# Decode attention with a gated feed-forward part: the heads' turning one wo block sooner, and the last wo row as two column halves

## The chip, the cores and the metric

The kernel runs on one core of a Trainium2 chip. The metric is the device time of one execution in microseconds (us); a lower time is better. Faster or slower needs 2%, which is 27 us here.

Two clocks occur below. The time of a run is 1.8 to 2.1 us longer than the span of its profile, which goes from the first to the last instruction. Moments in the text are microseconds from the span's start.

## The reference, cut to what matters

```python
q = (x @ wq).reshape(B, Sq, H, Dh).transpose(0, 2, 1, 3)      # B=4, Sq=1, D=1024, H=32, Dh=128
scores = jnp.einsum("bhqd,bhkd->bhqk", q, k_cache) * (Dh ** -0.5)   # k_cache: 4 x 32 x 8192 x 128
p = softmax(scores, axis=-1)
o = jnp.einsum("bhqk,bhkd->bhqd", p, v_cache)
a = o.transpose(0, 2, 1, 3).reshape(B, Sq, H * Dh) @ wo       # wo: 4096 x 1024
b = ...                                                       # a gated feed-forward part on x, 1024 -> 3584 -> 1024
out = g * a + (1 - g) * b
```

All data is bf16. The K and V caches are 268 MB each, so 576 MB have to come from memory for four rows of output.

## The kernel before

A ring of five slots holds K, V and weight tiles on their way from memory. V is used in pairs of pieces; behind the last V pair of a batch the sums `OS` of eight heads must be *turned* (rows to columns, by matmuls against a selector), scaled into `OT`, and *spread* by `o_rows` into `LT`, the form in which they are multiplied by wo. wo (8 MB) comes in eight blocks of 1 MB. Blocks 0 to 5 need only heads whose turning is long done; blocks 6 and 7 need the heads of the last V pair.

```python
def wo_block(g, r0=0, r1=FR):                 # starts the transfer of rows r0..r1 of block g
    home, at = divmod(g, 4)
    ...
    nc.sync.dma_start(out=w[:, r0:r1]..., in_=wov[:, g, r0:r1]...)

    def use():                                # and gives back the matmuls on it
        for r in range(r0, r1):
            for n in range(NH):               # NH = 2 column halves of 512
                mm_acc(n, LT[:, r, g, :], w[:, r, n * NB:(n + 1) * NB])
    return use
```

The program's last stage, with the numbers put in: blocks 2 to 5 are whole, block 6 comes in two halves of its rows, block 7 as rows 0-1, row 2, row 3.

```python
last = [wo_block(g) for g in range(2, NWB - 2)]            # NWB = 8
cuts = [(NWB - 2, 0, 2), (NWB - 2, 2, 4), (NWB - 1, 0, 2), (NWB - 1, 2, 3), (NWB - 1, 3, 4)]
last += [wo_block(*cut) for cut in cuts]
flush_sums()
for g in range(2, GE):                                     # GE = 6
    last.pop(0)()                                          # the matmuls of block g
    if g == 3:
        flush()                                            # the turning (8 matmuls, "led<-selg,OS")
        flush_late()                                       # OT, on VectorE
    if g == 4:
        o_rows(GE, NWB)                                    # the spreading (16 small matmuls, then LT on VectorE)
for use in last:
    use()                                                  # blocks 6 and 7
```

Two casts (VectorE for columns 0-511, ScalarE for 512-1023) and two output transfers follow.

## Time and profile before

| | before |
|---|---|
| median of the first three runs | 1343.41 us (1343.31 to 1343.79) |
| span of the profiled run | 1341.4 us |
| TensorE matmuls busy | 1057.9 us, 79% |
| VectorE busy | 638.3 us, 48% |
| read from memory | 575.68 MB, 429 GB/s over the span |
| tail: last transfer of block 5 landed, to the last cast's start | 1332.65 to 1338.37 = 5.72 us |

The lines of the page, of the chain and of the timeline that matter stand in the prediction. How to read them: busy tenths show which resource is never idle; the chain says which landing or engine released each step at the end; in the timeline the bracket tells how long an engine stood idle before a group and what ended it.

### The profile page before, as it was taken

How to read it: one execution, taken by the hardware profiler on the slowest of the kernel's cores; microseconds unless marked ns; L12 is line 12 of the kernel's file. 1: busy time of each engine (PE TensorE's matmuls, PEld its weight loads, DVE VectorE, ACT ScalarE, POOL GpSimd, SP SyncE). 2: the span in 40 equal slices, each digit the busy share in tenths (PEclk: the TensorE clock that was granted, in tenths of full speed). 3: DMA queues.
4: the chain of work that ended last, by engine and by line, in shares of the span. 5: the costliest groups of instructions: out<-in, count | busy, mean ns of one | idle time of the engine just before them, and what ended most of it. 6: DMA issues, size and time to landing. Idle time of an engine off the chain costs nothing.

```text
span 1341.4 us, 6922 instructions
## 1 busy us (share of the span) xinstructions
PE 1057.9 (79%) x4608; PEld 138.4 (10%) x1396; DVE 638.3 (48%) x386; ACT 66.2 (5%) x99; POOL 71.8 (5%) x209
## 2 busy tenths in 40 slices
PE   2565877887778789787879778789697879888888
PEld 0000000001001010101001010101011011111111
DVE  2555988556544347454436256646145556100000
ACT  0000000200000000100000000100000000111000
POOL 2000000100000001000000000100000000100000
PEclk9777989898989898888899888889898889889989
DMA  9999999999999999999999999999999999999998
GB/s 415 434 434 436 435 436 424 445 425 428 436 436 427 440 434 423 442 428 434 438 427 434 432 436 434 434 430 423 436 431 439 436 421 441 430 427 430 427 427 335
DMA packets 14890, 576.13 MB, mean 429 GB/s; under 512 B 1662, under 2 KB 1670, under 8 KB 2316
## 3 DMA queue, kind: packets, MB, share of 16 engines
q1 hardware_dynamic: 14852, 575.69, 99.5%
q8 instruction: 23, 0.38, 0.1%
q14 instruction: 7, 0.06, 0.0%
q10 hardware_dynamic: 8, 0.00, 0.0%
HBM read 575.68 MB, written 0.01 MB: 429 GB/s over the span
## 4 chain that ended last, share of the span: by engine, by line
DMA 67%; DVE 21%; PE 11%; issue 0%; ACT 0%; SPq 0%; DVEq 0%
DMA ring<-in_A_k_cache_dram 51%; DVE TB L453 19%; DMA ring<-in_A_v_cache_dram 12%; PE o_ps L537 7%; PE S_ps L458 3%; DMA ring<-in_B_w_gate_dram 3%; DVE OS L558 2%; DMA ring<-in_A_wo_dram 1%; PE o_ps L320 0%; DVE PT L494 0%; DVE mx L480 0%; PE acc L286 0%; PE led L574 0%; PE o_ps L574 0%; DVE OS L566 0%
## 5 line engine op out<-in xcount | busy, mean ns | idle before, releaser
L453 DVE STREAM_TRANSPOSE TB<-ring 128x2048 uint32<-128x2048 uint32 x256 | 568.3, 2278 | 472.6 <-DMA ring<-in_A_k_cache_dram 464.5
L458 PE MATMUL S_ps<-TB,Z 128*128 128x512 bf16 x2048 | 532.6, 415 | 191.4 <-DVE TB L453 183.6
L537 PE MATMUL o_ps<-ring,PB 128*64 128x512 bf16 x2048 | 462.8, 388 | 50.3 <-DMA ring<-in_A_v_cache_dram 49.0
L458 PEld LDWEIGHTS <-Z 128*128 128x128 bf16 x512 | 53.1, 104 | 656.0 <-issue 656.0
L537 PEld LDWEIGHTS <-PB 128*64 128x64 bf16 x512 | 57.1, 112 | 449.1 <-issue 446.4
L513 POOL COPY PB<-PT 32x256 bf16<-32x256 bf16 x64 | 39.1, 611 | 712.5 <-PE o_ps L537 519.4
L566 DVE SCALAR_TENSOR_TENSOR OS<-o_ps,mE,OS 128x512 f32<-128x512 f32 x5 | 3.8, 750 | 138.9 <-ACT OS L564 138.9
L511 ACT COPY PB<-PT 32x256 bf16<-32x256 bf16 x64 | 39.6, 619 | 256.8 <-PE o_ps L537 251.0
L435 POOL COPY Z<-qa 32x4 bf16<-32x4 bf16 x128 | 25.8, 201 | 459.8 <-PE S_ps L458 432.2
L554 ACT ACTIVATE OS<-o_ps,mE 128x512 f32<-128x512 f32 x11 | 7.6, 687 | 450.9 <-PE o_ps L537 450.9
L558 DVE SCALAR_TENSOR_TENSOR OS<-o_ps,mE,OS 128x512 f32<-128x512 f32 x33 | 24.3, 737 | 1.5
L489 ACT ACTIVATE TB<-S_ps,mx 128x2048 bf16<-128x2048 f32 x4 | 7.9, 1967 | 331.6 <-DVE mx L486 331.6
L286 PE MATMUL acc<-ring,hT 128*4 128x512 bf16 x56 | 14.7, 432 | 5.4 <-ACT TB L489 5.4
L244 PE MATMUL S_ps<-identb,x 6*128 6x6 bf16 x8 | 0.6, 196 | 22.5 <-DMA x<-in_gate_w_dram 22.5
L286 PE MATMUL acc<-ring,LT 128*4 128x512 bf16 x64 | 14.8, 378 | 1.9 <-DMA ring<-in_A_wo_dram 1.2
L574 PEld LDWEIGHTS o_ps<-selg,OS 128*128 128x128 f32 x88 | 11.5, 191 | 9.3 <-issue 8.8
L494 DVE STREAM_TRANSPOSE PT<-TB 128x2048 bf16<-128x2048 bf16 x4 | 9.2, 2311 | 6.4 <-ACT TB L489 6.4
L480 DVE TENSOR_REDUCE mx<-S_ps 128x1 f32<-128x2048 f32 x4 | 9.1, 2282 | 6.2 <-PE S_ps L458 6.2
L320 PE MATMUL o_ps<-ring,xw 128*4 128x512 bf16 x112 | 9.0, 444 | 3.7 <-DMA ring<-in_B_w_gate_dram 3.7
L574 PE MATMUL o_ps<-selg,OS 128*128 128x8 f32 x88 | 10.5, 245 | 0.0
L586 DVE SCALAR_TENSOR_TENSOR OT<-led,sgb,rinv 128x8 bf16<-128x8 f32 x5 | 1.2, 236 | 19.1 <-PE led L574 19.0
L564 ACT ACTIVATE OS<-o_ps,mE 128x512 f32<-128x512 f32 x5 | 3.4, 687 | 128.9 <-PE o_ps L537 128.9
(73 smaller groups left out, 83.0 us busy)
## 6 DMA issues: line engine op xcount, KB each, us to landing
ring<-in_A_v_cache_dram SPq DMA_DIRECT2D x18, 4096.0 KB, 28.9
ring<-in_A_k_cache_dram SPq DMA_DIRECT2D x14, 4096.0 KB, 30.9
ring<-in_A_v_cache_dram SPq DMA_DIRECT2D x6, 2048.0 KB, 40.0
ring<-in_B_w_gate_dram SPq DMA_DIRECT2D x1, 7168.0 KB, 37.1
ring<-in_B_w_up_dram SPq DMA_DIRECT2D x1, 7168.0 KB, 37.1
ring<-in_B_w_down_dram SPq DMA_DIRECT2D x1, 7168.0 KB
ring<-in_A_wo_dram SPq DMA_DIRECT2D x6, 1024.0 KB, 19.8
ring<-in_A_v_cache_dram SPq DMA_DIRECT2D x4, 1024.0 KB, 28.3
```

Source lines behind the costliest of these rows:

```text
L286: nc.tensor.matmul(acc(n), lhsT=lhsT, rhs=rhs, start=start, stop=True, skip_group_check=True)
L320: nc.tensor.matmul(ps[32 * k:32 * k + Bn, z, :], lhsT=xT[TW * half + t], rhs=cols(w, t, 4 * z + k), start=(half + t == 0), stop=(half == 1 ...
L435: nc.gpsimd.tensor_copy(out=Z[at, :, QP - 1 + QP * q], in_=qa[at, :, h0 + q, b])
L453: nc.vector.transpose(out=flat_t.bitcast(U32).rearrange("p (j i) -> p j i", j=CJ), in_=kn[:, half].bitcast(U32))
L458: nc.tensor.matmul(sps[:, z, :], lhsT=Z[:, 2 * half + e, s:s + P], rhs=T[:, 16 * z:16 * z + 16, :, e], start=(t + n + half + e == 0), stop ...
L480: nc.vector.tensor_reduce(out=mx[:, 0:1], in_=sps[:].rearrange("p z n -> p (z n)"), axis=AX.X, op=ALU.max)
L494: nc.vector.transpose(out=PT[:].rearrange("p j i -> p (j i)"), in_=PTs)
L511: nc.scalar.copy(out=Bv[at, :, :, q, :], in_=Pv[at])
L513: nc.gpsimd.tensor_copy(out=Bv[at, :, :, q, :], in_=Pv[at])
L537: nc.tensor.matmul(o_ps[w // 2][row:row + NM, w % 2, :], lhsT=PB[:, RD * (d % NW) + n, z].rearrange("p w s j -> p (w s j)"), rhs=vn[:, j0 ...
L558: nc.vector.scalar_tensor_tensor(out=OS[:], in0=o_ps[w // 2][:, w % 2, :], scalar=mE[:, w:w + 1], in1=OS[:], op0=ALU.mult, op1=ALU.add)
L574: nc.tensor.matmul(oT, lhsT=OS[:, q * Dh:(q + 1) * Dh], rhs=selg[:, q].rearrange("p t s -> p (t s)"), start=(q == 0), stop=(q == 3), skip_ ...
```

## The change

The turning is to come off TensorE's path in front of the last blocks; and the very last transfer is halved, so that one of the last two matmuls need not wait for the other's columns.

```diff
-    def wo_block(g, r0=0, r1=FR):
+    def wo_block(g, r0=0, r1=FR, half=None):
 ...
+        if half is None:
             nc.sync.dma_start(...)            # as before
+        else:
+            nc.sync.dma_start(out=w[:, r0, half * NB:(half + 1) * NB], in_=wov[:, g, r0, half * NB:(half + 1) * NB])
 ...
-                for n in range(NH):
+                for n in range(NH) if half is None else [half]:
 ...
-    cuts = [(NWB - 2, 0, 2), (NWB - 2, 2, 4), (NWB - 1, 0, 2), (NWB - 1, 2, 3), (NWB - 1, 3, 4)]
+    cuts = [(NWB - 2, 0, 2), (NWB - 2, 2, 4), (NWB - 1, 0, 2), (NWB - 1, 2, 3)] + [(NWB - 1, 3, 4, n) for n in range(NH)]
 ...
-        if g == 3:
+        if g == 2:
             flush()
             flush_late()
-        if g == 4:
+        if g == 3:
             o_rows(GE, NWB)
```

More of the change, by code (lines that the diff above doesn't have):

```diff
@@ L392, in wo_block @@
         w = wo_home[home][:, at]
-        nc.sync.dma_start(out=w[:, r0:r1].rearrange("p r n -> p (r n)"),
-                          in_=wov[:, g, r0:r1].rearrange("p r n -> p (r n)"))
+        if half is None:
+            nc.sync.dma_start(out=w[:, r0:r1].rearrange("p r n -> p (r n)"),
+                              in_=wov[:, g, r0:r1].rearrange("p r n -> p (r n)"))
+        else:
+            nc.sync.dma_start(out=w[:, r0, half * NB:(half + 1) * NB], in_=wov[:, g, r0, half * NB:(half + 1) * NB])
         def use():
             for r in range(r0, r1):
-                for n in range(NH):
+                for n in range(NH) if half is None else [half]:
                     mm_acc(n, LT[:, r, g, :], w[:, r, n * NB:(n + 1) * NB])
```

## The prediction

> **What bounds the kernel now.** I read the page from the top, then the chain that ended last for the final 100 us, then the timeline of the last 20 us. On the page the data transfers are the one thing that is busy throughout:
>
> ```profile
> PE   2565877887778789787879778789697879888888
> DMA  9999999999999999999999999999999999999998
> GB/s 415 434 434 436 435 436 424 445 425 428 436 436 427 440 434 423 442 428 434 438 427 434 432 436 434 434 430 423 436 431 439 436 421 441 430 427 430 427 427 335
> ```
>
> Each digit is the busy share of a fortieth of the span. DMA stands at 9 in 39 of 40 slices; TensorE never does twice running. The change touches none of this: it lies behind the last V pair, so only the last slices can move, and there I ask what the chain hangs on:
>
> ```profile
> 1293.15 27.07 DMA ring<-in_A_v_cache_dram
> ...
> 1320.28 16.12 DMA ring<-in_A_wo_dram
> 1336.40 0.04 issue
> 1336.44 1.90 PE acc L286 x8
> 1338.35 0.02 issue
> 1338.37 0.57 ACT TB L637
> ```
>
> Columns: start, duration, what. The end is released by a wo transfer issued at 1320.28 and landed at 1336.40; eight matmuls, one cast and the output follow, to 1341.4. The timeline shows the same stretch on TensorE, with the wait before each group in brackets:
>
> ```profile
> 1325.22 1.89 PE L286 MATMUL acc<-ring,LT 128*4 128x512 bf16 x8 [0.60 <-DMA ring<-in_A_wo_dram]
> ...
> 1326.40 0.69 DVE L568 TENSOR_TENSOR OS<-OS,TB 128x512 f32<-128x512 f32 x1
> ...
> 1327.72 1.89 PE L286 MATMUL acc<-ring,LT 128*4 128x512 bf16 x8 [0.61 <-DMA ring<-in_A_wo_dram]
> ...
> 1329.54 1.06 PE L574 MATMUL led<-selg,OS 128*128 128x8 f32 x8
> ...
> 1330.52 1.89 PE L286 MATMUL acc<-ring,LT 128*4 128x512 bf16 x8
> 1330.63 0.24 DVE L586 SCALAR_TENSOR_TENSOR OT<-led,sgb,rinv 128x8 bf16<-128x8 f32 x1 [3.54 <-PE led L574]
> ...
> 1332.25 0.33 PE L381 MATMUL led<-OT,identb 128*32 128x8 bf16 x16
> ...
> 1332.69 5.64 PE L286 MATMUL acc<-ring,LT 128*4 128x512 bf16 x24
> ```
>
> Blocks g = 2 and 3 (1325.22 and 1327.72) wait for their weights. Then come the heads' turning (L574), block 4, the spreading of the heads (L381), and blocks 5, 6, 7 as 24 matmuls from 1332.69. Those 24 are not gapless: single matmuls of the trace start 0.216 us apart, so 16 of them end at 1332.69 + 16 x 0.216 = 1336.14, and the chain says that the last eight began at 1336.44, 0.04 after a landing. TensorE was ahead of the data there by 0.3 us.
>
> The issue-to-landing view of the wo line, taken one issue at a time, gives the landings (issue plus time to landing):
>
> ```profile
> DMA to landing us min/median/max: 19.8/19.8/19.8
> DMA to landing us min/median/max: 18.6/18.6/18.6
> DMA to landing us min/median/max: 17.3/17.3/17.3
> DMA to landing us min/median/max: 16.1/16.1/16.1
> DMA to landing us min/median/max: 14.3/14.3/14.3
> ```
>
> With issues at 1312.8, 1315.3, 1317.8, 1320.3 and 1322.8 these are 1332.6 (block 5), 1333.9 and 1335.1 (halves of block 6), 1336.4 (rows 0-1 of block 7) and 1337.1 (row 2). The last row, row 3, has no entry since nobody was seen to wait for it; the trace's raw semaphore events, which no view prints, put row 2's last mark at 1337.04 and row 3's at 1337.68.
>
> **What the Trainium skill says.** (1) "DMA: Bandwidth & Descriptors", section "Why a DMA increments its semaphore by 16 and not by 1": one transfer runs on up to 16 engines that finish independently, and only all 16 marks mean that it has landed. The trace agrees: row 3's sixteen marks come between 1332.68 and 1337.68, so the slowest engine alone sets each landing. (2) Same page, "Specifications": rows of 512 B or more run at line rate. The halves have rows of 1 KB, so they should not fall off it; in the trace a packet of 4 KB took 159 ns, of 2 KB 84 ns, and of 1 KB (the output's) 47 ns, which is about 9 ns and 37 ns per KB. (3) Same page, "Anatomy of one DMA — SWDGE (gpsimd) path": of some 2 us fixed cost most is the write's receipt. That section is on another issuing path; here, from the end of the last 2 KB packet (1337.26) to the mark (1337.68) the trace has 0.42 us, and it is a latency that successive transfers overlap: row 3's mark comes only 0.64 us after row 2's. (4) "TensorE: Matmul & The Clock Gate", section "Wait — 56ns, not 53.3ns?": 215.7 ns between matmuls of 512 columns at full clock. The trace has 0.216 us in the tail, where the granted clock is 1.00.
>
> **The change, part by part.**
>
> *The turning sooner.* No instruction is added or removed on TensorE, VectorE, ScalarE or GpSimd (the instruction listings have equal counts, 3364 rows on TensorE); eight L574 matmuls (four in the source, each run as two) and sixteen L381 matmuls move up by one block of eight. Walked forward with measured durations: block 2 starts at 1325.22 as now and ends at 1325.22 + 8 x 0.216 = 1326.95. The turning needs OS, which L568 finishes at 1326.40 + 0.69 = 1327.09, so it starts about 1327.15 and takes 0.98 (1329.54 to 1330.52), to 1328.13. Block 3, landed at 1327.68, now starts 0.4 us later than before, 1328.13 to 1329.86. Meanwhile L586 makes OT by about 1328.5, so the L381 matmuls follow at once, 0.2 us, to 1330.06. Block 4 waits for its landing (raw event 1330.16), runs 1330.20 to 1331.93, against 1330.52 before. Block 5 landed at 1332.65: it starts at 1332.69, exactly as before. So 0.3 us is won at block 4 and all of it is waited away before block 5. LT for blocks 6 and 7, ready at 1332.84 before and needed at 1334.42, is ready two microseconds sooner than needed: also nothing. Sum of this part: 0.00 us.
>
> *The row in two halves.* One transfer of 256 KB becomes two of 128 KB: one more issue (0.33 us on SyncE's queue, which is idle from 1325.6 to 1338.9) and 8 more packets per engine. The second half's issue waits, by the listing, for the completion of the transfer eight before it, now block 3 (1327.68) instead of block 2 (1325.20); it is on the queue by 1328, and the fastest engine gets to it only after 1332. On the slowest engine row 3 cost 8 x 80 ns = 0.64 us between marks. In halves, with 47 - 4 = 43 ns a packet (I take off the 4 ns by which spacing is below duration for the 2 KB ones), each half takes 0.34: landings at 1337.38 and 1337.73. Needed by TensorE: rows 0-1 start at 1336.44, four matmuls to 1337.30, row 2 to 1337.74, then column half 0 at 1337.74 and half 1 at 1337.95. Before, row 3 landed at 1337.68, with only 0.06 to spare; after, the spare is 0.36 for the first half and 0.22 for the second. The last eight matmuls run gapless before and after, released by rows 0-1 at 1336.40. Sum of this part: 0.00 us in an execution like the profiled one; if the last row came late by d, at most min(d, 0.2) us won.
>
> Both parts buy slack where none is spent. Total: 0.0 us, with a small tilt to a gain, which I put at 0.1 us: 1343.41 - 0.1 = 1343.3.
>
> **The rivals.**
>
> *TensorE is the bound of the tail, and the moved turning comes off it.* Then up to the 0.98 of L574 plus 0.25 of L381 would be won, 1342.2. For it: from 1327.72 to 1332.4 TensorE is without a gap. Against: it waits for data at 1332.69 and again at 1336.44, both behind the moved work.
>
> *The last row's landing is the bound.* Spare is 0.06 us in the profiled run, and other runs may have less. Then the column halves let one matmul (0.216 us) go ahead: 1343.2.
>
> *The small transfers cost more than their bytes.* If a 1 KB packet took the 84 ns of a 2 KB one, the last half would land at 1337.04 + 2 x 0.64 = 1338.32 and the last matmul would start 0.41 us late: 1343.8. The output's 47 ns packets speak against it, though those are writes and not reads.
>
> *The earlier part shifts by itself.* Three runs of one program spread over 0.48 us; another program's queue phases could differ by as much with no cause in the change.
>
> **Range and chances.** The mechanisms above span 1342.2 to 1343.8; with the scatter of 0.5 us either way but the extremes unlikely, I take 1342.4 to 1344.1 for 8 in 10. Two per cent is 27 us, while the whole stretch behind the last V weights is 17 us (1324.5 to 1341.4): 0.99 for within 2%, half a per cent on each side, for a slow execution or a fault.
>
> **What would show it.** Right: block 5 starts within 0.1 us of its landing, with a new wait of 0.5 to 0.8 us for wo data before it; the chain still goes from a wo transfer through about eight L286 matmuls of 1.9 us to the cast; L574 stands between blocks 2 and 3 with L381 after block 3. Wrong on the first part: no data wait on TensorE between L381 and the end, and a span shorter by about 1 us. Wrong on the second: the chain's last wo transfer is a half row with one or two matmuls behind it, with the last landing later than 1337.95. The prediction as a whole fails if the V and K stages, which do not change, run differently by over 1 us.

## The result, and the profile after

The changed kernel took 1343.78 us (median of six runs, 1343.24 to 1344.11), the kernel before 1343.24 us (six runs, 1343.07 to 1343.79). The ratio is 1.0003 with a 95% interval of 0.999 to 1.0016: the same.

The chain of the changed kernel that ended last (start, duration, what):

```profile
1293.62 27.07 DMA ring<-in_A_v_cache_dram
...
1320.75 16.12 DMA ring<-in_A_wo_dram
1336.87 0.04 issue
1336.91 1.90 PE acc L286 x8
1338.81 0.02 issue
1338.83 0.57 ACT TB L640
```

It is the chain of before, piece by piece with the same durations, only 0.47 us later throughout. The same wo transfer (block 7, rows 0-1) releases it, and the same eight matmuls follow without a gap.

The timeline of the changed kernel's tail (start, duration, engine, line, operation, count, in brackets the idle time before):

```profile
1325.70 1.89 PE L286 MATMUL acc<-ring,LT 128*4 128x512 bf16 x8 [0.60 <-DMA ring<-in_A_wo_dram]
...
1327.61 1.06 PE L577 MATMUL led<-selg,OS 128*128 128x8 f32 x8
...
1328.60 1.89 PE L286 MATMUL acc<-ring,LT 128*4 128x512 bf16 x8
...
1330.33 0.32 PE L381 MATMUL led<-OT,identb 128*32 128x8 bf16 x16
...
1330.68 1.89 PE L286 MATMUL acc<-ring,LT 128*4 128x512 bf16 x8
1330.73 0.19 DVE L383 CAST LT<-led 128x32 bf16<-128x32 f32 x1 [1.78 <-PE led L381]
...
1333.18 5.62 PE L286 MATMUL acc<-ring,LT 128*4 128x512 bf16 x24 [0.61 <-DMA ring<-in_A_wo_dram]
```

The turning now stands between blocks 2 and 3, and the spreading between 3 and 4. What TensorE gained by that it waits for in front of block 5: the wait of 0.61 us there is new, and the 0.61 us that it used to wait in front of block 3 is gone. The bracketed waits for wo data add up to 1.2 us before and after. LT for blocks 6 and 7 is ready at 1330.92, 4.0 us before its first use at 1334.90; before, it was ready at 1332.84 and used at 1334.42.

Taking each kernel's own landing of block 5 (1332.65 and 1333.13) as zero, the last cast starts at 5.72 us before and 5.70 us after. So the tail did not change, and the 0.47 us between the two traces had arisen before the tail began. Every engine that drives that earlier part runs an unchanged instruction stream. Comparing the two traces instruction by instruction, the distance between them wanders: 0.0 us at 200 us, -0.3 at 280, +0.5 at 430, 0.0 at 600, +0.45 at 900, 0.0 at 1100, +0.47 at 1325.

The second half of the last row landed at 1338.19, and TensorE reached its matmul at 1338.42. (Landings of single rows, and starts of single matmuls, are read from the raw events of the traces, which no view prints.)

### The profile page after: what moved, and what is told of

Same layout as the page of the kernel before. It is cut to its first block, busy times and chain, and to the rows that moved or that the text cites. A ratio compares the mean times of both kernels' runs of the same rounds, so it can differ in the third digit from the quotient of the medians.

```text
span 1341.8 us, 6924 instructions
## 1 busy us (share of the span) xinstructions
PE 1059.8 (79%) x4608; PEld 138.4 (10%) x1396; DVE 638.5 (48%) x386; ACT 66.2 (5%) x99; POOL 71.4 (5%) x209
## 4 chain that ended last, share of the span: by engine, by line
DMA 66%; DVE 20%; PE 11%; another core or an unknown queue 1%; issue 0%; SPq 0%; DVEq 0%; ACT 0%
DMA ring<-in_A_k_cache_dram 51%; DVE TB L456 18%; DMA ring<-in_A_v_cache_dram 12%; PE o_ps L540 7%; PE S_ps L461 4%; DVE OS L561 2%; DMA x<-in_gate_w_dram 2%; DMA ring<-in_A_wo_dram 1%; PE S_ps L320 0%; PE o_ps L320 0%; DVE PT L497 0%; DVE mx L483 0%; PE acc L286 0%; PE led L577 0%
```

## The experiments

My theory: TensorE's tail is paced by landings, each of which is set by the slowest of 16 DMA engines; both parts of the change widen a slack that was not used up, so they are worth 0.0 us; the rest is scatter from upstream. The rivals: TensorE is the tail's bound (then part one pays about 1 us); the last landing is the bound (then part two pays 0.2 us); small transfers cost extra (then part two costs 0.2 to 0.5 us); the change itself costs the half microsecond between the medians.

Eleven runs were made, each with the kernel before at its side; p0, e9 and e10 repeat the kernel before, the changed kernel and e7. All gave correct results. "Tail" is the stretch defined above, read from each trace: landing of block 5 to the last cast's start. A *mark* is one of the sixteen semaphore updates, one from each DMA engine, that together say that a transfer has landed.

| run | tail, us | median, us | before, us | ratio (95% interval) |
|---|---|---|---|---|
| before / after, first comparison | 5.72 / 5.70 | 1343.78 (after) | 1343.24 | 1.0003 (0.999 to 1.0016) |
| p0_again | 5.70 | 1343.17 | 1343.22 | 1.0 (0.9987 to 1.0012) |
| e1_turn_only | 5.73 | 1343.46 | 1343.22 | 1.0001 (0.9988 to 1.0015) |
| e2_halves_only | 5.70 | 1343.36 | 1343.22 | 1.0001 (0.9987 to 1.0014) |
| e3_turn_two_late | 7.55 | 1345.01 | 1343.22 | 1.0013 (0.9998 to 1.0029) |
| e4_turn_one_late | 6.37 | 1343.98 | 1343.31 | 1.0006 (0.9991 to 1.0021) |
| e5_block7_whole | 6.91 | 1344.41 | 1343.31 | 1.001 (0.9995 to 1.0024) |
| e6_single_rows | 5.74 | 1343.02 | 1343.31 | 0.9999 (0.9984 to 1.0014) |
| e7_rows_and_halves | 5.53 | 1342.94 | 1343.31 | 0.9997 (0.9981 to 1.0014) |
| e9_after_again | 5.70 | 1343.17 | 1343.49 | 1.0 (0.9987 to 1.0012) |
| e10_rows_and_halves_again | 5.53 | 1342.91 | 1343.49 | 0.9997 (0.9983 to 1.0011) |
| e8_more_fetches | 5.70 | 1346.22 | 1343.49 | 1.002 (1.0006 to 1.0034) |

The intervals are some 0.13% wide to each side, 1.7 us. No experiment on the tail can be decided by them; the traces decide, and the medians are only looked at for contradiction.

### The control

The kernel before, unchanged.

> The kernel before once more, unchanged, as a control. Own theory (the half microsecond between the medians is scatter from upstream: instruction fetches that hit one DMA engine or another): its median differs from that of the kernel before on this chip by up to 0.5 us in either direction, its interval contains 1, and the profiled execution's spread between the first and the last engine's mark of the last row is again between 5 and 6 us (5.0 before, 5.7 to 5.8 after). Rival (the change itself costs some 0.5 us): two runs of the same program agree within 0.2 us. Tail, from block 5's landing to the last cast's start: 5.72 us as before (5.70 after).

Its median is 0.05 us from that of the kernel before, with runs from 1343.02 to 1343.72. The last row's marks spread over 4.90 us, from the first engine to the last, where I expected 5 to 6. Medians within 0.2 us of each other are what the rival expected too, so the control does not decide between the two; e9 below does that. The tail measure repeats to 0.02 us, so differences of 0.1 us in it can be read.

### Each part alone

e1 has only the moved turning, e2 only the halved row:

```diff
 # e1_turn_only, against before (turning, then spreading)
-        if g == 3:
+        if g == 2:
-        if g == 4:
+        if g == 3:
 # e2_halves_only, against after
-        if g == 2:
+        if g == 3:
-        if g == 3:
+        if g == 4:
```

> Part one alone: the turning one block sooner, the last row whole. Own theory (slack only): the tail from block 5's landing to the last cast's start stays 5.72 us within 0.05, with a data wait of 0.6 us before block 5, and the time is the kernel before's within 0.5 us. Rival (TensorE is the tail's bound): tail shorter by up to 1 us.

> Part two alone: the last row as two column halves, the turning where it was. Own theory: tail 5.72 us within 0.05, the last half's mark 0.6 to 0.7 us behind row 2's and 0.2 us before TensorE needs it. Rival (small transfers cost a fixed sum each): last mark 1.0 us or more behind row 2's and the tail longer by 0.2 to 0.5 us.

Tails of 5.73 and 5.70 us: neither part does anything, and there are no two effects that cancel. In the timeline of e1 the last group of 24 matmuls shows the wait that takes up the gain:

```profile
1332.38 5.65 PE L286 MATMUL acc<-ring,LT 128*4 128x512 bf16 x24 [0.60 <-DMA ring<-in_A_wo_dram]
```

In e2 row 2's last mark came at 1336.84, those of the halves at 1337.17 and 1337.49: 0.33 and 0.32 us a half, 0.65 for the row. Two transfers cost what one did. TensorE began the last matmul at 1337.72, 0.23 us after the last mark. The rival of the costly small transfer is out.

### The turning moved the other way

If the tail has slack for the turning, using it up must show at some point, and from then on one for one.

```diff
 # e4_turn_one_late, against before
-        if g == 3:
+        if g == 4:
             flush()
             flush_late()
-        if g == 4:
+        if g == 5:
             o_rows(GE, NWB)
 # e3_turn_two_late, against before
-        if g == 3:
+        if g == 5:
             flush()
             flush_late()
-        if g == 4:
             o_rows(GE, NWB)
```

> The turning one block later than the kernel before (after block 4, spreading after block 5), the last row whole. Own theory: block 5 starts at about 0.3 us after its landing, LT is ready some 1 us too late for block 6, tail 5.72 + 0.7 = 6.4 us. Rival (data alone): tail 5.7 us.

> The turning moved the other way: after block 5, with the spreading straight behind it (two blocks later than the kernel before), the last row whole. Own theory (the order costs nothing until the slack is used up, then one for one): blocks 6 and 7 wait for LT, their 16 matmuls start some 1.9 us late, tail 5.72 + 1.9 = 7.6 us, no data wait behind block 5, and the time is up by 1.5 to 2.3 us. Rival (the tail hangs on the data whatever the order): tail 5.7 us.

The tails came out at 6.37 and 7.55 us, against 6.4 and 7.6 expected, and the medians rose by 0.67 and 1.79 us. The timelines of e4 (one line) and of e3 say how:

```profile
1335.15 3.62 PE L286 MATMUL acc<-ring,LT 128*4 128x512 bf16 x16 [0.32 <-DVE LT L383]
```

```profile
1334.17 1.06 PE L574 MATMUL led<-selg,OS 128*128 128x8 f32 x8
1335.56 0.34 PE L381 MATMUL led<-OT,identb 128*32 128x8 bf16 x16 [0.33 <-DVE OT L586]
1336.21 3.61 PE L286 MATMUL acc<-ring,LT 128*4 128x512 bf16 x16 [0.32 <-DVE LT L383]
```

In both, blocks 6 and 7 now wait for LT from VectorE and no longer for data; all 16 matmuls stand behind it. So the order of TensorE's work does matter in this tail. It had merely been set right already: one block later than before costs 0.65 us, one block sooner than before brings nothing.

### The cuts of block 7

```diff
 # e5_block7_whole, against before
-    cuts = [(6, 0, 2), (6, 2, 4), (7, 0, 2), (7, 2, 3), (7, 3, 4)]
+    cuts = [(6, 0, 2), (6, 2, 4), (7, 0, 4)]
 # e6_single_rows, against after
-    cuts = [(6, 0, 2), (6, 2, 4), (7, 0, 2), (7, 2, 3), (7, 3, 4, 0), (7, 3, 4, 1)]
+    cuts = [(6, 0, 2), (6, 2, 4), (7, 0, 1), (7, 1, 2), (7, 2, 3), (7, 3, 4)]
 # e7_rows_and_halves, against after
-    cuts = [(6, 0, 2), (6, 2, 4), (7, 0, 2), (7, 2, 3), (7, 3, 4, 0), (7, 3, 4, 1)]
+    cuts = [(6, 0, 2), (6, 2, 4), (7, 0, 1), (7, 1, 2), (7, 2, 3), (7, 3, 4, 0), (7, 3, 4, 1)]
```

(6 and 7 stand for `NWB - 2` and `NWB - 1`, and the loops over rows and halves are written out.)

> Block 7 as one transfer, uncut; the turning as before. Own theory (the slowest engine's end is fixed by the bytes, the cuts decide how many matmuls stand behind it): all eight matmuls wait for the last mark, tail 5.72 + 1.28 = 7.0 us, time up by 1.0 to 1.6 us. Rival (cuts are hidden anyway): tail 5.7 us.

> The changed kernel with block 7 in four single rows, the last row whole. Own theory: TensorE is now ready for the last row 0.3 us before it lands, so the last row's landing binds instead of rows 0-1: tail 5.71 us, unchanged, with a wait for wo data before the last two matmuls. Rival (every extra transfer costs time): tail longer by 0.1 us or more.

> As the run with four single rows, with the last row in column halves as in the changed kernel. Own theory: only here can the halves pay, one matmul (0.2 us) goes ahead of the last landing: tail 5.5 us, 0.2 shorter than with single rows and than both kernels; the time still cannot be told from theirs. Rival (halves never pay): tail 5.7 us.

With block 7 uncut the tail grew to 6.91 us. All eight matmuls stand behind the last landing, 1.33 us of waiting, in the timeline of e5:

```profile
1337.59 1.89 PE L286 MATMUL acc<-ring,LT 128*4 128x512 bf16 x8 [1.33 <-DMA ring<-in_A_wo_dram]
```

I had 7.0. The uncut block landed 2.47 us after the last half of block 6 (1335.08 to 1337.55) where the kernel before needed 2.53 for its three transfers.

With four single rows TensorE is further along when the last row arrives, and then it is that row's landing that binds. The chain of e6:

```profile
1331.46 6.45 PE acc L286 x29
1337.91 0.04 issue
1337.95 0.61 PE acc L286 x2
1338.55 0.02 issue
1338.58 0.58 ACT TB L640
```

The view names no transfer here. The single matmuls do: they start 0.216 us apart up to row 3, and there the step is 0.416 us, 0.20 of it a wait that ended 0.04 us after the row's last mark (1337.90). Only two matmuls are left behind this release, not eight, and yet the tail is 5.74: the finer rows moved the bound from rows 0-1 to row 3 without a gain. Now, and only now, do the halves pay. e7 adds them and the tail falls to 5.53 us, by the length of one matmul, 0.216. The chain of e7:

```profile
1314.03 19.82 DMA ring<-in_A_wo_dram
1333.85 0.04 issue
1333.89 5.47 PE acc L286 x24
1339.36 0.02 issue
1339.38 0.58 ACT TB L641
```

It now runs from block 5's landing through 24 matmuls with hardly a gap. 24 x 0.216 = 5.18 us of the 5.47 is their pace, the rest their latency and two gaps of 0.1 us or less, so TensorE itself has become nearly the bound and finer cuts have almost nothing left to win. This is the version that the experiments point to, and so it ran once more beside the changed kernel:

> The version with four single rows and the last in halves once more, since its trace had the shortest tail and its profiled execution the longest span. Own theory: tail 5.5 us again; the median is 0.2 to 0.4 us below the kernel before's, too little to be told from it. Rival: the tail's gain does not show in the median at all.

> The changed kernel once more, five rounds. Own theory (the first comparison's half microsecond was scatter): the median is within 0.4 us of the kernel before's, tail from block 5's landing to the last cast 5.70 us, last half landing 0.2 us before TensorE needs it. Rival (the change costs some 0.5 us): again 0.4 to 0.6 us above.

The tails repeat: 5.53 and 5.70. The median of e10 is 0.58 us below that of the kernel before, of e7 0.37 below. The traces account for some 0.35 us: 0.19 in the tail, and 0.15 to 0.16 behind the last cast, where the stretch to the end shrank from 3.03 us to 2.88 (e7) and 2.87 (e10; see the last section). The 0.37 fits that; the 0.58 exceeds it, and lies outside the 0.2 to 0.4 expected. Two of e10's five runs are at 1343.86 and 1343.99, and the intervals contain 1: it beats both kernels in the trace, and is the same in the time. The changed kernel's own median was this time 0.32 us *below* that of the kernel before, after +0.54 in the first comparison. The rival by which the change costs half a microsecond has the second comparison and the 0.02 us of the tail against it. One thing stays unexplained: in the profiled executions of the four kernels with both parts (after, e7, e9, e10) block 5 landed at 1333.13 to 1333.85, in the other eight with the same number of instruction fetches at 1332.31 to 1332.84. The medians of e7, e9 and e10, all below the kernel before's, show no such cost, so it may be chance; no run tests it.

### Where the scatter comes from

Twelve profiled executions (before, after, and all runs but e8) differ in when block 5 lands, from 1332.31 (e3) to 1333.85 us (e7), though the transfers issued up to there are the same. The sixteen marks of the last transfer tell where it arises: I took for each execution how far the slowest engine's mark lies behind the middle of the sixteen. It is 1.76 us in e3, 1.98 before, 2.62 after, 3.05 in e9, and 3.23 in e7; against the landing of block 5 the twelve points have a correlation of 0.99 and a slope of 1.0. An execution is late by what its slowest DMA engine is late.

Following the marks through one trace, they start within 0.3 us of each other, and single marks fall behind in steps. In e3, the first transfer to land after the instruction fetch at 43 us has one mark at 1.8 us where the others stay within 0.4; after the one at 101 us there are two such marks, and so on, until at 1315 us seven of the 16 are 4.4 to 4.7 us behind the first. The fetch of 16 KB of instructions takes 0.97 to 1.11 us in e3's transfer records, and a mark steps about 1.4 us back. Where just one fetch lies between two whole transfers of e3, the sixteen lags behind the first mark grew together by 1.2 to 2.2 us in 18 of 19 cases; where none does, typically by 0.0 and at most by 1.0. An engine that has fallen behind does not catch up: no place in e3's order of marks came closer to the first by more than 0.22 us. That fits transfers dealt out in equal parts: in the kernel before each mark of row 3 comes 0.62 to 0.66 us behind one of row 2. In e3 the last mark is three such steps behind, in e7 four.

To test this I left the repeated weight loads in, so that TensorE's instruction stream is 3212 instructions longer:

```diff
 # e8_more_fetches, against before
-    nc.at_finalize(keep_weights)
```

> The kernel before with every repeated weight load left in, to test where the scatter comes from: some 3200 more TensorE instructions. Own theory: the traces show that each fetch of 16 KB of instructions puts one of the 16 DMA engines 1.4 us behind for good, and the engine that is hit most often ends the kernel; with 23 fetches now and 12 or 13 more, the first-to-last spread of the last row's marks goes on growing in steps of 1.4 us or stays at 4.5 to 6, the whole set of marks shifts, and the time rises by 1 to 2 us. Rival (fetches are unrelated): 23 fetches or no change of the marks' steps at the extra fetches. Confounded: TensorE has more work, so the steps of the marks decide and not the time.

The transfer counts of the kernel before and of e8 (queue, kind: packets, MB, share):

```profile
q8 instruction: 23, 0.38, 0.1%
```

```profile
q8 instruction: 36, 0.59, 0.2%
```

Thirteen fetches more; the time rose by 2.73 us, more than the 1 to 2 expected. The tail is 5.70 us as ever, so all of it arose upstream. The last mark of the last row came 2.83 us later than before, the first mark 0.64 us later, and the spread grew from 4.99 to 7.18 us in further steps of 1.3 to 1.7. With 23 fetches it lay between 4.56 (e3) and 6.05 us (e9), so 1.1 us of the widening is beyond what the other executions show. The steps fall at the fetches: with one fetch between two transfers, the sixteen lags grew together by 1.4 to 2.4 us in 21 of 22 cases, with none typically by 0.0 and at most by 1.1. So fetches are a source of the lag. How much of the 2.73 us they cost remains open: the weight loads also kept TensorE busier (472 us of weight loading instead of 138), and the profile of the kernel before that I compare with is from another chip. Which engine serves which fetch the trace does not record, I made no kernel that has the scatter taken away, and why the last mark steps back three times in one execution and four in another is not shown.

## Why the prediction was right

Against the predicted 1343.3 us (1342.4 to 1344.1) stand 1343.78 in the first comparison and 1343.17 in the second. The steps, with the 0.47 us by which the whole tail was later in the trace taken off:

- *The turning*: start predicted 1327.15, measured 1327.14; block 3 at 1328.13, measured 1328.13; the spreading behind block 3 at 1329.86, measured 1329.86; block 4 at 1330.20, measured 1330.21. The predicted new wait of 0.5 to 0.8 us before block 5 was 0.61, and block 5 started 0.05 after its landing. One reading was off: the prediction has LT ready two microseconds sooner than needed, and it was 4.0; it mattered to nothing. (Both traces have 4608 matmuls and 1396 weight loads.) e1 shows the sum of 0.00 for this part alone.
- *The halves*: 0.34 us each predicted, 0.31 and 0.32 measured; spare time 0.36 and 0.22 predicted, 0.33 and 0.23 measured. The 47 ns of a 1 KB packet, taken from the output's writes, held for these reads as well (median 46). e2 shows the sum of 0.00 for this part alone.
- *TensorE as the bound*: excluded by the wait before block 5, and by e1. e3 and e4 show that the turning, with VectorE's share in it, would have been the bound one or two blocks later.
- *The last landing as the bound*: in e6 it is, and there the step's 0.2 us appears (e7); in the two kernels compared it is not.
- *Dear small transfers*: excluded by e2.
- *The upstream shift*: this was the weakest step. I named it as a rival of 0.5 us without a cause and still tilted the sum to a gain of 0.1 us. The first comparison had +0.54 us, the second -0.32, and one of the runs of e9 lies 1.3 us above the median of its own kernel. The size is near the step of one instruction fetch on the slowest engine, which fits but is not shown run by run. The tilt had no ground in the tail either: the measured difference there is 0.02 us, within what the control repeats. Behind the last cast 0.06 us more were saved (3.03 to 2.97), for a reason that the prediction did not have. So the mechanism was right by the traces; how near the time itself came to 1343.3 is luck within the scatter.

## What to carry to other kernels

Before moving work away from the path that sets the end, walk the new order forward against the landings: a gain that ends in front of the same landing is worth nothing, and the bracketed waits of the timeline say in advance where it will end. Cutting the last transfer finer paid only where that transfer's landing was the last release in the chain; here the chain was released by rows 0-1 with all eight matmuls of block 7 behind them, and only cutting those rows too made the halves worth their one matmul. When a kernel is limited by data, differences below the reach of the slowest DMA engine's scatter, here 1.5 us, are to be read from a stretch of the trace that starts behind the scatter, and not from the median.

## What the Trainium skill lacked or had wrong

- "Runtime: NRT & Kernel Launch", section "Instruction fetch mechanics", gives 16 KiB blocks, which the trace confirms, and says that crossing a boundary costs a tail-bump, "mostly hidden". It lacks what a fetch costs a kernel limited by data: at the fetches single marks stepped about 1.4 us back and stayed there, the slowest ended 1.8 to 3.2 us behind the middle, and 13 more fetches came with 2.73 us more time (with TensorE busier too).
- "DMA: Bandwidth & Descriptors", section "Where 436 GB/s comes from", says without a condition that the memory side, some 358 GB/s, binds for transfers between HBM and the core. This kernel, whose program ran on one core only, read at 429 GB/s over its whole span, in line with that page's own 16 MB measurement of 425 GB/s with one core at work.
- The same page, section "Anatomy of one DMA — SWDGE (gpsimd) path", has a fixed cost of some 2 us; no page has the time from a load's last data packet to its mark when SyncE issues it. Here such a load had its last mark 0.42 us after its last data packet, and a transfer behind another did not pay even that: marks of successive transfers of 128 and 256 KB came 0.3 to 0.7 us apart, by their bytes. Packets of 1, 2 and 4 KB took 46, 84 and 159 ns, so halving 2 KB rows cost next to nothing (0.61 to 0.67 us a row in the five traces with halves, 0.62 to 0.65 in those with a whole last row).
- No page has the closing checks: with one transfer more, the stretch from the last cast to the end shrank from 3.03 to 2.97 us (after, e2, e6), and with two more to 2.88 (e7), while kernels with the old count (p0, e1, e3, e4) kept 3.03; e5, with two fewer, had 2.93, so it is not the count as such. In the traces SyncE checks the completion marks one after another, 0.06 to 0.07 us each, and with more transfers the output's marks came later in that row. I read the shift from the traces and did not test it apart.
